# A mixing kernel for one core: the leftover group of the middle stage on 96 rows and 128 columns

## The chip, the cores and the metric

The kernel runs on one core of a Trainium2 chip. The metric is the time of one execution on the device in microseconds, of which the median over several runs is compared. The engines are named as in the profile: PE (TensorE, matmuls; PEld are its weight loads), DVE (VectorE), ACT (ScalarE), POOL (GpSimd) and SP (SyncE, which here only issues DMAs).

## What is computed

The first half is a global filter: a real Fourier transform along the sequence of 3008 positions, a product with a complex filter, and the way back, for 8 batches and 256 channels. The second half is a feed-forward layer with the activation h - tanh(h).

```
batch, seq, dim = (8, 3008, 256)          # d_ff = 2048
X = np.fft.rfft(x, axis=1)
F = (filt_r + 1j * filt_i)[None, :, :]
y = np.fft.irfft(X * F, n=x.shape[1], axis=1)
h = y.reshape(8 * 3008, 256) @ w_in
out = (h - np.tanh(h)) @ w_out
```

## The kernel before

3008 is 64 x 47, and the transform goes in stages. For every batch a *first* stage (`first`) multiplies by 64-point matrices and stores to `ct1` in HBM; a *middle* stage (`middle`) loads from `ct1`, does the 47-point transform, the filter and the 47-point way back, and stores to `ct2`; a *last* stage (`last`) loads from `ct2` and multiplies by 64-point matrices again, 128 columns a matmul, into `ut`. From there `up`, `shrink` and `down` are the feed-forward layer, whose matmuls (lines L469 and L639) are by far the most.

The middle stage has 32 slots of 24 rows each (`NA`, `NH`: frequencies of one residue), 4 planes and 256 channels. Slots are taken in groups of five, `SLOTS`, so there are six groups of 5 x 24 = 120 rows (`KM`) and one leftover group, the seventh, of 2 x 24 = 48 rows (`KL`). A group's way through the stage:

- `load_a2` and `load_ft` load its data (`a2`, line L270) and its filter rows (`ft`, L276), both on SP's queue, while the group ahead is worked on.
- `forth`: twice two matmuls (L287) of the group's matrices, as weights, with 256 columns of `a2`, into a PSUM bank `pa`; ACT copies the first bank (L290), DVE adds and subtracts (L292, L293).
- `filtered`: six DVE operations over four planes or two (L303, L318, L320, L321, L323, L324). For batch 0 some of it runs in another form (`pool` is given).
- `back`: twice two matmuls (L334) into a bank `pe`, a copy by ACT to `e1` (L337), and a store to `ct2` that ACT issues itself (L338).

The matrices lie in `mats`. For the groups of five they are block diagonal with five equal 24x24 blocks. The leftover group holds the slots 30 and 31, of which the last is the special one of the frequencies 0 and half; its eight matrices have two different blocks, and stand 48 columns wide (`KL`) behind the others. `ways` picks them.

The order of the work is written out by hand. The feed-forward runs in quarters `U`: `up` of one, `shrink` of the one before and `down` of the one before that are interleaved. Within it `up` calls `t(k)`, which puts in one step of the generators `first` and `middle` of later batches at planned positions (`planned`), and a PSUM bank of the feed-forward is borrowed for it (`zd`, bank "y" or "t"). So the matmuls of the middle stage stand singly in the stream of PE, between those of `up` and `down`. On the borrowed bank "y" they follow the DVE operation L492, which reads that bank. One batch's period is 24 such quarters.

Batch 0 isn't handled there: in the prologue its middle stage is unrolled, with `forth`, `filtered` and `back` called with the functions' 256 columns (`there0`, `ended`). The prologue also loads `mats`, its first three matrices on SP's queue and the rest with one issue on POOL's queue (L968), between the loads of the filter rows of the first two groups (`filters_of`), ahead of two small copies (`turned_rows`) and of weight loads (L143).

Of the kernel before, what the change touches and what calls it, by code (L numbers as in the profile page):

```python
# [9 lines left out]
F32 = mybir.dt.float32  # L10
# [7 lines left out]
BATCH, SEQ, DM = 8, 3008, 256  # L18
# [10 lines left out]
SLOTS = [(a, min(SG, NA - a)) for a in range(0, NA, SG)]  # L29
KM = SG * NH  # L30
KL = SLOTS[-1][1] * NH

SMALL = 0.36
FACTORS = [(0.28138768672943115, 0.18210311233997345, 0.5012423992156982),
# [12 lines left out]
def _consts():  # L47
    q = np.arange(NQ)[:, None]
    k1 = np.arange(1, NA)[None, :]

    def angle(r):
        return 2 * np.pi * ((k1 * (NR * q + r)) % SEQ) / SEQ

    def sign(r):
        return (-1.0) ** ((q[:, 0] + r) % 2)

    f = np.zeros((2, NQ, NH, 4, NA))
    g = np.zeros((4, NA, NH, 2, NQ))
    for r in range(NH):
        for half, n in ((0, r), (1, NR - r)):  # L60
            if half and not r:
                continue
            odd = 1.0 - 2 * half
            c, s = np.cos(angle(n)), np.sin(angle(n))
            f[half, :, r, 0, :-1], f[half, :, r, 1, :-1] = c, -s
            f[half, :, r, 2, :-1], f[half, :, r, 3, :-1] = -odd * s, odd * c
            plus, minus = (1 + sign(n)) / 2, (1 - sign(n)) / 2
            f[half, :, r, 0, -1], f[half, :, r, 2, -1] = plus, minus
            f[half, :, r, 1, -1], f[half, :, r, 3, -1] = odd * plus, odd * minus
            g[0, :-1, r, half], g[1, :-1, r, half] = 2 * c.T, -2 * s.T  # L70
            g[2, :-1, r, half], g[3, :-1, r, half] = -2 * odd * s.T, 2 * odd * c.T
            g[0, -1, r, half], g[2, -1, r, half] = plus, minus
            g[1, -1, r, half], g[3, -1, r, half] = odd * plus, odd * minus
    g /= SEQ

    t = 2 * np.pi * (np.outer(np.arange(NH), np.arange(NH)) % NR) / NR
    cos, sin = np.cos(t), np.sin(t)
    twice = np.where(np.arange(NH) > 0, 2.0, 1.0)[:, None]
    mats = np.zeros((KM, 6 * KM + 8 * KL))
    for k, m in enumerate((cos, sin, -sin)):  # L80
        way = np.einsum("rm,st->srmt", m, np.eye(SG))
        mats[:, k * KM:k * KM + KM] = way.reshape(KM, KM)
        mats[:, (3 + k) * KM:(4 + k) * KM] = way.reshape(KM, KM).T
    for k, (a, b) in enumerate(((cos, cos), (cos, -sin), (sin, cos), (-sin, -sin),
                                (cos, twice * cos), (cos, -2 * sin),
                                (sin, twice * cos), (-sin, -2 * sin))):
        at = 6 * KM + k * KL
        mats[0:NH, at:at + NH], mats[NH:KL, at + NH:at + KL] = a, b

    f = f[:, :, :, ORDER, :]  # L90
    return [np.ascontiguousarray(v, dtype=np.float32)
            for v in (f.reshape(128, -1), f[:, :, :, 0:2].reshape(128, -1), g.reshape(128, -1), mats, np.eye(128))]

@with_exitstack
def kernel(
# [24 lines left out]
    def dram(t, off, dims):  # L120
        return bass.AP(tensor=t, offset=off, ap=[list(d) for d in dims])

    mats = cst.tile([KM, 6 * KM + 8 * KL], F32, name="mats_sb")
    groups = [(b, c) for b in range(BATCH) for c in range(NC)]
    count = cst.tile([1, 1], I32, name="count")
    one = cst.tile([128, 128], F32, name="one_sb")

    def ways(g, back):

        if g < len(SLOTS) - 1:  # L130
            m = [mats[0:KM, (3 * back + k) * KM:(3 * back + k + 1) * KM] for k in range(3)]
            return m[0], m[0], m[1], m[2]
        at = 6 * KM + 4 * back * KL
        return [mats[0:KL, at + k * KL:at + (k + 1) * KL] for k in range(4)]

    wu = cst.tile([128, 7, DFF // 2], F32, name="wu")
    wd = cst.tile([128, 7, DFF // 2], F32, name="wd")
# [119 lines left out]
            ACT.dma_start(dram(ct1[b], XH * c * DM, [[NH * DM, 128], [1, XH * DM]]), a1)  # L257
            yield

    def rows(t, b, g, first_block=0, n=4):  # L260

        a, s = SLOTS[g]
        return dram(t[b], (first_block * NA + a) * NH * DM,
                    [[DM, s * NH], [NA * NH * DM, n], [1, DM]])

    def load_a2(b, g, tag="a2", bufs=2):

        n = SLOTS[g][1] * NH
        t = tr.tile([KM, 4, DM], F32, tag=tag, bufs=bufs, name="a2")
        nc.sync.dma_start(t[0:n], rows(ct1, b, g))  # L270
        return t

    def load_ft(g):
        n = SLOTS[g][1] * NH
        t = tr.tile([KM, 4, DM], F32, tag="ft", bufs=2, name="ft")
        nc.sync.dma_start(t[0:n], dram(filt_d, g * KM * 4 * DM, [[4 * DM, n], [1, 4 * DM]]))  # L276
        return t

    def forth(g, at, z):

        n = SLOTS[g][1] * NH
        xy = tr.tile([KM, 4, DM], F32, tag="xy", bufs=2, name="xy")[0:n]
        way = ways(g, 0)
        for v in (1, 0):
            pa = z("pa", [128, 2, DM])[0:n]
            for k in range(2):
                nc.tensor.matmul(pa[:, k], way[2 * v + k], at[0:n, PLACE[2 * v + k]],  # L287
                                 start=True, stop=True)
            if v:
                ACT.copy(xy[:, 2:4], pa)  # L290
            yield xy
        V.tensor_add(xy[:, 0:2], pa, xy[:, 2:4])  # L292
        V.tensor_sub(xy[:, 2:4], pa, xy[:, 2:4])  # L293
        yield

    def filtered(g, xy, ft, by, by2, pool=None):

        n = SLOTS[g][1] * NH
        ab = xy.rearrange("p (x v) c -> p x v c", v=2)
        fv = ft[0:n].rearrange("p (x v) c -> p x v c", v=2)  # L300
        nn = (tr.tile([128, 4, DM], F32, tag="nn", bufs=1, name="nn") if pool is None else
              pool.tile([KM, 4, DM], F32, tag="nn", bufs=3, name="nn"))[0:n]
        by.tensor_mul(nn.rearrange("p (x v) c -> p x v c", v=2), ab,  # L303
                      fv[:, :, 0:1].to_broadcast([n, 2, 2, DM]))
        yield nn
        if pool is not None:
            fi = ft[0:n, 1:4:2]
# [10 lines left out]
        by.tensor_mul(ab, ab, fv[:, :, 1:2].to_broadcast([n, 2, 2, DM]))  # L318
# [5 lines left out]
        V.tensor_sub(xy[:, 2:4], nn[:, 0:2], nn[:, 2:4])  # L324
        yield

    def back(b, g, xy, z):

        n = SLOTS[g][1] * NH
        way = ways(g, 1)  # L330
        for v in range(2):
            pe = z("pe", [128, 2, DM])[0:n]
            for k in range(2):
                nc.tensor.matmul(pe[:, k], way[2 * v + k], xy[:, 2 * v + k],  # L334
                                 start=True, stop=True)
            e1 = tr.tile([128, 2, DM], F32, tag="e1", bufs=2, name="e1")[0:n]
            ACT.copy(e1, pe)  # L337
            ACT.dma_start(rows(ct2, b, g, 2 * v, 2), e1)  # L338
            yield

    def middle(b, z):
# [495 lines left out]
    with tc.tile_pool(name="tr", bufs=2) as tr, tc.manual_schedule():  # L837
# [12 lines left out]
        with tc.tile_pool(name="pro", bufs=1) as pro, \  # L850
# [60 lines left out]

            def back0(g, nn):

                way = ways(g, 1)
                for v in range(2):
                    pe = z0("pe", [128, 2, DM])[0:KM]
                    for k in range(2):
                        nc.tensor.matmul(pe[:, k], way[2 * v + k], nn[:, k],
                                         start=True, stop=False)
                        nc.tensor.matmul(pe[:, k], way[3 - k if v else 0], nn[:, 2 + k],  # L920
                                         start=False, stop=True)
                    e1 = pro.tile([128, 2, DM], F32, tag="e1", bufs=5, name="e1")[0:KM]
                    ACT.copy(e1, pe)
                    ACT.dma_start(rows(ct2, 0, g, 2 * v, 2), e1)

            def tiles0(k, dtype, n):
                return pro.tile([128, n], dtype, tag=k, name=k,
# [37 lines left out]
            G.tensor_copy(gate, xs[1][64:65, 0, 0:1])  # L965
            began.append(begun(tiles0, jobs[2], queue=G))
            fts = {0: filters_of(0)}
            G.dma_start(mats[:, 3 * KM:], mats_d[:, 3 * KM:])  # L968
            fts[1] = filters_of(1)
            turned_rows()  # L970

            early = weights(tiles0, range(3), G, began, 3)
# [32 lines left out]
            summed = (last_g,)  # L1005

            def there0(g):
                there = forth(g, a2.pop(g), z0)
                xy = next(there)
                next(there)  # L1010
                return there, xy
# [12 lines left out]
            for g in range(last_g + 1):  # L1024
# [14 lines left out]
                    next(chain)  # L1039
                if g in summed:  # L1040
                    next(chain)
                ended.append((back, (0, g, xy, z0)) if g in summed else (back0, (g, nn)))
                if g:
                    way_back()
                if g == last_g - 1:
# [192 lines left out]
```

## Time and profile before

| what | value |
|---|---|
| median of 3 runs | 2751.55 us (2750.81 to 2753.89) |
| the profiled execution | 2753.31 us, its span 2751.4 us |
| TensorE clock granted, mean of the span | 0.996 |
| DMA queue of SP | 293981 packets, 146.89 MB, 21.9% of 16 engines |
| DMA queue of ACT | 39056 packets, 48.25 MB, 5.8% |
| matrices' load on POOL's queue | one issue, 348.8 KB, landed after 8.4 us |
| a load of the leftover group (a2, ft) | 192 KB each, 7 and 7 issues |
| a store of the leftover group | 96 KB, 16 issues (batch 0 included) |

In the profile's groups an entry names the line, the engine, the operation, what is written from what, then the shape: for a matmul first rows\*columns of the weights, then partitions x columns of the result. After the bar stand the busy time and the mean of one instruction, and after the second bar the idle time of the engine in front of it and what ended it. In a timeline a line has the start and the length in us, and how many instructions were merged (x4). Lengths of matmuls overlap, since one starts before the last has left the array; what one costs is the distance from its start to the next start.

### The profile page before, as it was taken

The page shows a single profiled execution, that of the slowest core. Times are in us where ns is not written, and L with a number is a line of the kernel's source. Part 1 is how long each engine was busy: PE and PEld are TensorE (multiplying, and loading weights), DVE is VectorE, ACT ScalarE, POOL GpSimd, SP SyncE. Part 2 cuts the span into 40 slices and gives each one's busy share as a digit, 9 for nine tenths or more (in the row PEclk, how much of TensorE's full clock was granted, in tenths as well). Part 3 has the DMA queues.
Part 4 walks back from the last instruction along what each step waited for, and adds up shares of the span by engine and source line. Part 5 has one row for each costly group of instructions (what it writes and reads, how often), then busy time and mean ns, then how long its engine had stood idle before and what let it go on. Part 6 is the DMA issues. An engine that isn't in the chain of part 4 may idle for free.

```text
span 2751.4 us, 36435 instructions
## 1 busy us (share of the span) xinstructions
PE 2706.0 (98%) x12934; PEld 2366.6 (86%) x12934; DVE 1669.0 (61%) x2082; ACT 1730.6 (63%) x2595; POOL 1296.8 (47%) x1070
## 2 busy tenths in 40 slices
PE   8899999999999999999999999999999999999998
PEld 7578889888898888988889888898888988899887
DVE  6667766666556665666646665466655666644545
ACT  3566666666666666666666666666666666666665
POOL 3115445544554454545455445455454554455452
PEclk9999999999999999999999999999999999999999
DMA  7753222331233312423233222332322221111110
GB/s 197 226 170 98 72 59 72 103 90 40 65 84 97 83 48 62 113 69 82 51 76 97 70 78 53 94 78 68 84 57 63 52 63 53 30 27 31 22 25 17
DMA packets 336508, 207.77 MB, mean 76 GB/s; under 512 B 226390, under 2 KB 299042, under 8 KB 336061
## 3 DMA queue, kind: packets, MB, share of 16 engines
q1 hardware_dynamic: 293981, 146.89, 21.9%
q10 hardware_dynamic: 39056, 48.25, 5.8%
q0 software_dynamic: 3280, 10.22, 1.3%
q8 instruction: 104, 1.70, 0.3%
q14 instruction: 87, 0.71, 0.1%
HBM read 133.31 MB, written 74.97 MB: 76 GB/s over the span
## 4 chain that ended last, share of the span: by engine, by line
PE 90%; DVE 4%; DMA 2%; issue 2%; ACT 2%; ACTq 0%; POOL 0%; SPq 0%; DVEq 0%; POOLq 0%
PE o L639 38%; PE x L469 22%; PE z L469 11%; PE y L469 5%; PE pa L287 3%; PE pu L431 3%; PE pe L334 3%; PE pf L255 2%; DMA raw<-in_moe_w_in_dram 1%; PE o L693 1%; DVE h L591 1%; DVE h L525 1%; DVE h L492 1%; DMA ct<-e 0%; DVE xy L324 0%
## 5 line engine op out<-in xcount | busy, mean ns | idle before, releaser
L639 PE MATMUL o<-t,wd 128*128 128x256 f32 (+1 forms) x3008 | 760.8, 376 | 0.0
L449 POOL TENSOR_TENSOR t<-h 128x512 f32<-128x512 f32 (+1 forms) x186 | 256.2, 1377 | 930.4 <-DVE h L591 857.7
L591 DVE TENSOR_TENSOR h<-h,y 128x1024 f32<-128x1024 f32 (+1 forms) x384 | 512.2, 1334 | 286.6 <-ACT y L587 286.0
L639 PEld LDWEIGHTS o<-t,wd 128*128 128x128 f32 x3008 | 571.3, 190 | 68.8 <-issue 2.4
L469 PE MATMUL x<-tu,wu 128*128 128x256 f32 (+1 forms) x2256 | 574.7, 377 | 1.7 <-ACT u L475 1.2
L639 PE MATMUL o<-h,wd 128*128 128x256 f32 (+1 forms) x2256 | 571.4, 376 | 1.8 <-DVE h L591 1.8
L469 PEld LDWEIGHTS x<-tu,wu 128*128 128x128 f32 x2256 | 422.3, 190 | 62.2 <-ACT u L475 9.8
L639 PEld LDWEIGHTS o<-h,wd 128*128 128x128 f32 x2256 | 424.7, 190 | 52.2 <-DVE h L591 2.6
L475 ACT COPY s<-x 128x512 f32<-128x512 f32 (+1 forms) x188 | 108.6, 578 | 501.4 <-PE x L469 486.5
L581 ACT ACTIVATE y<-h 128x1024 f32<-128x1024 f32 (+1 forms) x384 | 400.1, 1042 | 14.3 <-ACT a L256 6.7
L584 ACT ACTIVATE y<-y 128x1024 f32<-128x1024 f32 (+1 forms) x384 | 399.2, 1039 | 12.1
L587 ACT ACTIVATE y<-y 128x1024 f32<-128x1024 f32 (+1 forms) x384 | 399.9, 1041 | 5.4 <-ACT a L256 0.8
L509 DVE TENSOR_TENSOR h<-z,u 128x512 f32<-128x512 f32 (+1 forms) x188 | 127.6, 678 | 258.4 <-ACT u L475 257.3
L475 ACT COPY u<-x 128x512 f32<-128x512 f32 (+1 forms) x376 | 214.7, 571 | 86.3 <-PE x L469 65.1
L451 POOL TENSOR_TENSOR t<-h 128x512 f32<-128x512 f32 (+1 forms) x186 | 266.9, 1435 | 0.0
L450 POOL TENSOR_TENSOR t<-h,t 128x512 f32<-128x512 f32 (+1 forms) x186 | 259.7, 1396 | 14.6
L452 POOL TENSOR_TENSOR t<-h,t 128x512 f32<-128x512 f32 (+1 forms) x186 | 263.4, 1416 | 0.0
L517 DVE COPY h<-x 128x512 f32<-128x512 f32 (+1 forms) x188 | 127.9, 680 | 157.9 <-PE x L469 157.3
L469 PE MATMUL z<-ut,wu 128*128 128x256 f32 (+1 forms) x752 | 190.4, 376 | 0.0
L469 PE MATMUL z<-tu,wu 128*128 128x256 f32 (+1 forms) x752 | 190.3, 376 | 0.0
L469 PE MATMUL x<-ut,wu 128*128 128x256 f32 (+1 forms) x752 | 190.2, 376 | 0.0
L469 PE MATMUL y<-ut,wu 128*128 128x256 f32 (+1 forms) x752 | 190.1, 375 | 0.0
(145 smaller groups left out, 3086.3 us busy)
## 6 DMA issues: line engine op xcount, KB each, us to landing
e<-ct SPq DMA_DIRECT2D x48, 512.0 KB
ct<-e ACTq DMA_DIRECT2D x96, 240.0 KB
ct<-a ACTq DMA_DIRECT2D x82, 256.0 KB
a<-ct SPq DMA_DIRECT2D x42, 480.0 KB
ft<-filt SPq DMA_DIRECT2D x42, 480.0 KB
out_dram<-ot SPq DMA_DIRECT2D x1248, 16.0 KB
x_sb<-in_x_dram SPq DMA_DIRECT2D x154, 128.0 KB
gt<-g SPq DMA_DIRECT2D x48, 256.0 KB
```

Of the source, the lines that this page charges most:

```text
L449: by.tensor_sub(t[0], b[0][1], b[0][0])
L450: by.tensor_sub(t[1], b[1][1], t[0])
L451: by.tensor_sub(t[2], b[1][1], b[0][1])
L452: by.tensor_sub(t[3], b[1][0], t[1])
L469: nc.tensor.matmul(bank[:, k], wu[:, q - 1, (2 * u + k) * 128:(2 * u + k + 1) * 128], rhs[q - 1], start=(first and k == 0), stop=True, ski ...
L475: ACT.copy(t, X)
L517: V.tensor_copy(h[:, 2, :, 0:w], X)
L581: ACT.activation(y[k], ht[k], AF.Arctan, scale=TURN)
L584: ACT.activation(y[k], y[k], AF.Tanh, scale=BEND)
L587: ACT.activation(y[k], y[k], AF.Square, scale=SCALE, accum_out=y_sums[:, 2 * U + k // 2:2 * U + k // 2 + 1])
L591: V.tensor_mul(ht[k], ht[k], y[k])
L639: nc.tensor.matmul(product(q), wd[:, q - 1, (2 * u + k) * 128: (2 * u + k + 1) * 128], rhs[q - 1][:, k], start=(u == 0 and k == 0 and q == ...
```

## The change

The leftover group of the batches 1 to 7 is laid out anew: the first 128 channels stand on 48 rows as before, and the second 128 channels on 48 further rows below. So its tiles have 96 rows (`KH`) and 128 columns instead of 48 and 256. Its matrices become 96x96 with the old 48x48 twice on the diagonal. Batch 0 keeps the old form (`whole`) with the upper left quarter of the new matrices. Each load of `a2` and `ft` and each store of `e1` of this group is issued in two halves of 128 channels, of 512 bytes a run. The load of the matrices on POOL's queue is split: the three matrices of the way back of the groups of five first, the leftover group's eight, now 96 rows of 768 columns, after the second group's filter rows. The number and the order of matmuls stay.

The core of the diff (lines of `_consts`, the helpers, the prologue):

```diff
+KH = 2 * KL
...
-    mats = np.zeros((KM, 6 * KM + 8 * KL))
+    mats = np.zeros((KM, 6 * KM + 8 * KH))
...
-        at = 6 * KM + k * KL
-        mats[0:NH, at:at + NH], mats[NH:KL, at + NH:at + KL] = a, b
+        for row in (0, KL):
+            at = 6 * KM + k * KH + row
+            mats[row:row + NH, at:at + NH] = a
+            mats[row + NH:row + KL, at + NH:at + KL] = b
...
+    def extent(g, whole):
+
+        n = SLOTS[g][1] * NH
+        return (n, DM) if whole or g < len(SLOTS) - 1 else (2 * n, DM // 2)
...
-        at = 6 * KM + 4 * back * KL
-        return [mats[0:KL, at + k * KL:at + (k + 1) * KL] for k in range(4)]
+        at = 6 * KM + 4 * back * KH
+        return [mats[0:n, at + k * KH:at + k * KH + n] for k in range(4)]
...
+    def parts(t, b, g, whole, first_block=0, n=4):
 
         a, s = SLOTS[g]
-        return dram(t[b], (first_block * NA + a) * NH * DM,
-                    [[DM, s * NH], [NA * NH * DM, n], [1, DM]])
+        rows, w = s * NH, extent(g, whole)[1]
+        for h in range(DM // w):
+            yield (slice(rows * h, rows * (h + 1)), w,
+                   dram(t[b], (first_block * NA + a) * NH * DM + w * h,
+                        [[DM, rows], [NA * NH * DM, n], [1, w]]))
...
-        nc.sync.dma_start(t[0:n], rows(ct1, b, g))
+        for rows, w, src in parts(ct1, b, g, False):
+            nc.sync.dma_start(t[rows, :, 0:w], src)
...
-        nc.sync.dma_start(t[0:n], dram(filt_d, g * KM * 4 * DM, [[4 * DM, n], [1, 4 * DM]]))
+        for h in range(DM // w):
+            nc.sync.dma_start(t[rows * h:rows * (h + 1), :, 0:w],
+                              dram(filt_d, g * KM * 4 * DM + w * h,
+                                   [[4 * DM, rows], [DM, 4], [1, w]]))
...
-                nc.tensor.matmul(pa[:, k], way[2 * v + k], at[0:n, PLACE[2 * v + k]],
+                nc.tensor.matmul(pa[:, k], way[2 * v + k], at[0:n, PLACE[2 * v + k], 0:w],
...
-            ACT.copy(e1, pe)
-            ACT.dma_start(rows(ct2, b, g, 2 * v, 2), e1)
+            ACT.copy(e1[0:n], pe)
+            for rows, _, dst in parts(ct2, b, g, whole, 2 * v, 2):
+                ACT.dma_start(dst, e1[rows])
...
-            G.dma_start(mats[:, 3 * KM:], mats_d[:, 3 * KM:])
+            G.dma_start(mats[:, 3 * KM:6 * KM], mats_d[:, 3 * KM:6 * KM])
             fts[1] = filters_of(1)
+            G.dma_start(mats[0:KH, 6 * KM:], mats_d[0:KH, 6 * KM:])
             turned_rows()
```

In `filtered` and `back` the tiles are cut to `n` rows and `w` columns in the same way.

More of the change, by code (lines that the diff above doesn't have):

```diff
@@ L121, in dram @@
         return bass.AP(tensor=t, offset=off, ap=[list(d) for d in dims])
-    mats = cst.tile([KM, 6 * KM + 8 * KL], F32, name="mats_sb")
+    mats = cst.tile([KM, 6 * KM + 8 * KH], F32, name="mats_sb")
     groups = [(b, c) for b in range(BATCH) for c in range(NC)]
@@ L126, with ways @@
     one = cst.tile([128, 128], F32, name="one_sb")
-    def ways(g, back):
+    def extent(g, whole):
+        n = SLOTS[g][1] * NH
+        return (n, DM) if whole or g < len(SLOTS) - 1 else (2 * n, DM // 2)
+    def ways(g, back, n):
         if g < len(SLOTS) - 1:
@@ L258, in first, with forth @@
             yield
-    def rows(t, b, g, first_block=0, n=4):
+    def parts(t, b, g, whole, first_block=0, n=4):
         a, s = SLOTS[g]
-        return dram(t[b], (first_block * NA + a) * NH * DM,
-                    [[DM, s * NH], [NA * NH * DM, n], [1, DM]])
+        rows, w = s * NH, extent(g, whole)[1]
[3 more added lines that the diff above has]
+                        [[DM, rows], [NA * NH * DM, n], [1, w]]))
     def load_a2(b, g, tag="a2", bufs=2):
-        n = SLOTS[g][1] * NH
         t = tr.tile([KM, 4, DM], F32, tag=tag, bufs=bufs, name="a2")
-        nc.sync.dma_start(t[0:n], rows(ct1, b, g))
+        for rows, w, src in parts(ct1, b, g, False):
+            nc.sync.dma_start(t[rows, :, 0:w], src)
         return t
     def load_ft(g):
-        n = SLOTS[g][1] * NH
+        n, w = extent(g, False)
+        rows = SLOTS[g][1] * NH
         t = tr.tile([KM, 4, DM], F32, tag="ft", bufs=2, name="ft")
-        nc.sync.dma_start(t[0:n], dram(filt_d, g * KM * 4 * DM, [[4 * DM, n], [1, 4 * DM]]))
-        return t
[L279 to L283, printed above, removed]
+        for h in range(DM // w):
+            nc.sync.dma_start(t[rows * h:rows * (h + 1), :, 0:w],
+                              dram(filt_d, g * KM * 4 * DM + w * h,
+                                   [[4 * DM, rows], [DM, 4], [1, w]]))
+        return t
+    def forth(g, at, z, whole=False):
+        n, w = extent(g, whole)
+        xy = tr.tile([KM, 4, DM], F32, tag="xy", bufs=2, name="xy")[0:n, :, 0:w]
+        way = ways(g, 0, n)
         for v in (1, 0):
-            pa = z("pa", [128, 2, DM])[0:n]
+            pa = z("pa", [128, 2, DM])[0:n, :, 0:w]
             for k in range(2):
-                nc.tensor.matmul(pa[:, k], way[2 * v + k], at[0:n, PLACE[2 * v + k]],
+                nc.tensor.matmul(pa[:, k], way[2 * v + k], at[0:n, PLACE[2 * v + k], 0:w],
                                  start=True, stop=True)
@@ L296, in filtered @@
     def filtered(g, xy, ft, by, by2, pool=None):
-        n = SLOTS[g][1] * NH
+        n, w = extent(g, pool is not None)
         ab = xy.rearrange("p (x v) c -> p x v c", v=2)
-        fv = ft[0:n].rearrange("p (x v) c -> p x v c", v=2)
+        ft = ft[0:n, :, 0:w]
+        fv = ft.rearrange("p (x v) c -> p x v c", v=2)
         nn = (tr.tile([128, 4, DM], F32, tag="nn", bufs=1, name="nn") if pool is None else
-              pool.tile([KM, 4, DM], F32, tag="nn", bufs=3, name="nn"))[0:n]
+              pool.tile([KM, 4, DM], F32, tag="nn", bufs=3, name="nn"))[0:n, :, 0:w]
         by.tensor_mul(nn.rearrange("p (x v) c -> p x v c", v=2), ab,
-                      fv[:, :, 0:1].to_broadcast([n, 2, 2, DM]))
+                      fv[:, :, 0:1].to_broadcast([n, 2, 2, w]))
         yield nn
         if pool is not None:
-            fi = ft[0:n, 1:4:2]
+            fi = ft[:, 1:4:2]
             V.tensor_mul(xy[:, 1:3], xy[:, 1:3], fi)
@@ L317, in filtered @@
             return
-        by.tensor_mul(ab, ab, fv[:, :, 1:2].to_broadcast([n, 2, 2, DM]))
+        by.tensor_mul(ab, ab, fv[:, :, 1:2].to_broadcast([n, 2, 2, w]))
         yield
@@ L325, in filtered, with back @@
         yield
-    def back(b, g, xy, z):
-        n = SLOTS[g][1] * NH
-        way = ways(g, 1)
+    def back(b, g, xy, z, whole=False):
+        n, w = extent(g, whole)
+        way = ways(g, 1, n)
         for v in range(2):
-            pe = z("pe", [128, 2, DM])[0:n]
+            pe = z("pe", [128, 2, DM])[0:n, :, 0:w]
             for k in range(2):
@@ L335, in back @@
                                  start=True, stop=True)
-            e1 = tr.tile([128, 2, DM], F32, tag="e1", bufs=2, name="e1")[0:n]
-            ACT.copy(e1, pe)
-            ACT.dma_start(rows(ct2, b, g, 2 * v, 2), e1)
+            e1 = tr.tile([128, 2, DM], F32, tag="e1", bufs=2, name="e1")[:, :, 0:w]
+            ACT.copy(e1[0:n], pe)
+            for rows, _, dst in parts(ct2, b, g, whole, 2 * v, 2):
+                ACT.dma_start(dst, e1[rows])
             yield
@@ L912, in back0 @@
             def back0(g, nn):
-                way = ways(g, 1)
+                way = ways(g, 1, KM)
                 for v in range(2):
@@ L923, in back0 @@
                     ACT.copy(e1, pe)
-                    ACT.dma_start(rows(ct2, 0, g, 2 * v, 2), e1)
+                    ACT.dma_start(next(parts(ct2, 0, g, True, 2 * v, 2))[2], e1)
             def tiles0(k, dtype, n):
@@ L1007, in there0 @@
             def there0(g):
-                there = forth(g, a2.pop(g), z0)
+                there = forth(g, a2.pop(g), z0, True)
                 xy = next(there)
@@ L1041 @@
                     next(chain)
-                ended.append((back, (0, g, xy, z0)) if g in summed else (back0, (g, nn)))
+                ended.append((back, (0, g, xy, z0, True)) if g in summed else (back0, (g, nn)))
                 if g:
```

## The prediction

> **What bounds the kernel now.** I read the page first, then the groups with different shapes kept apart, then PE's timeline around the instructions that the change touches, and last the waits. The page:
>
> ```profile
> span 2751.4 us, 36435 instructions
> PE 2706.0 (98%) x12934; PEld 2366.6 (86%) x12934; DVE 1669.0 (61%) x2082; ACT 1730.6 (63%) x2595; POOL 1296.8 (47%) x1070
> PE 90%; DVE 4%; DMA 2%; issue 2%; ACT 2%; ACTq 0%; POOL 0%; SPq 0%; DVEq 0%; POOLq 0%
> ```
>
> TensorE is the bound: busy 98% of the span and 90% of the chain, no other engine over 63%. So an edit is worth what it takes from PE's stream of matmuls, plus what it takes from a wait of PE. The groups by form:
>
> ```profile
> L431 PE MATMUL pu<-gt,e 128*128 128x128 f32 x736 | 99.2, 278 | 4.2 <-DMA e<-ct 4.2
> L334 PE MATMUL pe<-xy,mats_sb 48*48 48x256 f32 x64 | 16.8, 385 | 1.0 <-DVE h L492 1.0
> L287 PE MATMUL pa<-a,mats_sb 48*48 48x256 f32 x64 | 16.8, 385 | 3.0 <-DVE h L492 3.0
> L324 DVE TENSOR_TENSOR xy<-nn 48x512 f32<-48x512 f32 x7 | 11.2, 1604 | 0.0
> L653 DVE TENSOR_TENSOR o<-o,p 128x256 f32<-128x256 f32 x40 | 17.0, 425 | 54.2 <-ACT p L652 54.2
> ```
>
> Each f32 matmul leaves two records: 64 of the 48-row form on each line are 8 batches x 4 matmuls x 2. The mean of 385 ns is latency; matmuls overlap, so cost is read from start to start. A 256-column group, a 120-row group of the middle stage, and the 128-column matmuls of the last stage, on PE's timeline:
>
> ```profile
> 959.72 1.03 PE L287 MATMUL pa<-a,mats_sb 120*120 120x256 f32 x4
> 960.58 1.03 PE L469 MATMUL x<-tu,wu 128*128 128x256 f32 x4
> 961.45 1.24 PE L639 MATMUL o<-t,wd 128*128 128x256 f32 x5
> ...
> 982.28 1.03 PE L469 MATMUL y<-ut,wu 128*128 128x256 f32 x4
> 983.14 1.05 PE L431 MATMUL pu<-gt,e 128*128 128x128 f32 x8
> 984.03 1.25 PE L639 MATMUL o<-h,wd 128*128 128x256 f32 x5
> ```
>
> Four records of 256 columns take 0.86 us, 216 ns each, 120 rows or 128. Eight of 128 columns take 0.89 us, 111 ns each. Now one leftover group (48 rows) in the stream:
>
> ```profile
> 1010.96 1.03 PE L469 MATMUL x<-ut,wu 128*128 128x256 f32 x4
> 1011.82 1.03 PE L469 MATMUL y<-ut,wu 128*128 128x256 f32 x4
> 1012.78 0.59 PEld L287 LDWEIGHTS pa<-a,mats_sb 48*48 48x48 f32 x4 [0.33 <-issue]
> 1012.78 1.06 PE L287 MATMUL pa<-a,mats_sb 48*48 48x256 f32 x4
> 1013.77 1.59 PEld L639 LDWEIGHTS o<-h,wd 128*128 128x128 f32 x8 [0.40 <-issue]
> 1013.77 2.00 PE L639 MATMUL o<-h,wd 128*128 128x256 f32 x8
> ...
> 1015.60 0.59 PE L469 MATMUL x<-tu,wu 128*128 128x256 f32 x2
> ```
>
> The y group before it takes 0.96 instead of 0.86, the group itself 0.99 instead of 0.86, and the eight records behind it 1.83 instead of 8 x 0.216 = 1.73. That is 0.33 us lost though nothing is waited for; record by record it is 0.325 us in every undisturbed leftover group. The weight loads stand still at both edges (0.33 and 0.40 "issue"), which they don't around the 120-row group. In the prologue eight transposes of form 128\*48 (128 rows, 48 columns) follow each other at 109 ns without such a gap, so the few rows cost it, not the few columns.
>
> The Trainium skill, page "TensorEngine Tiling (Array Packing)", section "Tiling Modes", says that the array can be split at 64 rows for small contractions and that changing the mode drains it. The gaps at both edges of 48 rows agree with that; by its list of modes 96 rows need the whole array, as 120 do.
>
> **The change part by part.** Seven batches x 4 groups (two L287, two L334) = 28 groups of 4 records, 112 records, turn from 48 rows x 256 columns to 96 x 128; their order on PE stays.
>
> (a) Columns: 112 x (216 - 111) ns = 11.7 us less. The 111 is from full 128x128 loads, the nearest row above; the shorter 96-column load (48\*48 loads take 119 ns on average, 120\*120 loads 183 to 186) can't be worse.
>
> (b) The edges: 28 x 0.325 = 9.1 us less if 96 rows behave like 120. No row shows 96; bounds are 0 (like 48) and 9.1 (like 120). I take 9.1, since the 120-row group lies nearer and the loss goes with rows. A correction: six of the groups start behind a DVE wait (once near 359 us, then near 666, 1001, 1336, 1671, 2006). There the wait hides the edge in front, and a 120-row group behind a wait shows its first load exposed (314 instead of 216 ns), so these save 0.13 instead of 0.325: -1.1 us.
>
> (c) DVE and one wait. The leftover group's DVE operations fall from 1024 and 512 elements a row to half. In five batches PE waits before the first back group:
>
> ```profile
> 1055.06 1.76 DVE L324 TENSOR_TENSOR xy<-nn 48x512 f32<-48x512 f32 x1
> 1056.75 0.67 DVE L492 TENSOR_TENSOR h<-y,s 128x512 f32<-128x512 f32 x1
> 1057.48 1.06 PE L334 MATMUL pe<-xy,mats_sb 48*48 48x256 f32 x4 [0.20 <-DVE h L492]
> ```
>
> L492 frees the bank, and it queues behind the group's L323 (0.67) and L324 (1.76). At 256 elements an undisturbed operation takes 0.425 (L653); L324 is stretched beside POOL's L450 and L451, by 1.76 / 0.68 = 2.6 over its undisturbed length, so at worst it becomes 0.425 x 2.6 = 1.1. L492 then starts at least (0.67 + 1.76) - (0.425 + 1.1) = 0.9 us earlier, more than the wait: the record in front lasts 585 ns there and 309 at an edge without a wait, 0.276 us. Five times: 1.4 us less. Bounds 0 and 1.4. The rest of what DVE gains, some 4 us a batch, pays nothing: no PE wait ends there. The waits near 971 and 1001 us (0.87 and 0.68) hang on 120-row operations and stay.
>
> (d) ACT. Per batch three copies shrink (0.58 to about 0.37, L652's 128x256), and each of the two stores becomes two issues: 14 more of 0.33 us. Behind the added issue on ACT stands the copy L475 of u (1059.64 to 1060.23), which the next matmuls into x (1062.02) wait for: 1.8 us of cover against 0.33 - 0.21 = 0.12 us. Without cover 14 x 0.33 = 4.6 us. Behind the prologue 98 such stores are issued; 96 start 0.03 us after their copy, two wait longer (0.49 and 1.79 us, at 260 and 270, while SP moves the filter rows). I take 0.
>
> (e) Loads on SP: a2 and ft of the group in two issues each, 14 more of 0.33 to 0.5 us, and runs of 512 B instead of 1 KB and 4 KB. They are issued a whole group ahead (at 942 and 947 for matmuls from 1001 on), and SP's queue mostly waits for its next store. The e2 load of the next batch waits for the group's stores: issued at 1069.18, first used at 1094, cover 25 us. 0; bounds 0 and 1 us a batch.
>
> (f) Prologue: the matrices' load on POOL's queue is split, its second part put behind batch 0's second filter, and grows from 349 KB in all to 169 + 288 = 457 KB. One POOL issue more (0.8 us) stands ahead of the two turned rows and two weight loads; POOL then sits idle 8.9 us until 43.47, and the new part is first needed near 68 us. I take 0; bounds -0.5 (the first part lands earlier) to 2 us.
>
> Sum: 11.7 + 9.1 - 1.1 + 1.4 = 21.1 us less. The first copy x of the next half after a group was free 3.0 us before it was written (1012.60 against 1015.60), so 0.75 us off a group doesn't run into ACT.
>
> The profiled execution took 2753.3 us with a span of 2751.4; the median of the three runs is 2751.55. The span should fall to 2730.3, the median to **2730.5**.
>
> **The rivals.** *The edges stay.* If the array is changed over for 96 rows too, (b) is gone: 11.7 + 1.4 = 13.1, or 2738.4. For it: no 96-row matmul is shown. Against it: 120 rows, which don't fill the array either, pay nothing.
>
> *Weight loads bind.* A load takes up to 190 ns; were each to last that long on the path, a record would cost 190, not 111: 112 x 79 ns = 8.8 us less gain, 2739.3. Against it stand 736 records of L431 at 111 ns with such loads. The Trainium skill, page "TensorE: Matmul & The Clock Gate", section "Back-to-back issue gap", gives 81 ns per 128-column matmul when loads alternate, against 56 for the array alone. By that a two-pass record would take an estimated 162 ns and the gain shrink by 5.7 us; the trace's 111 is twice the smaller figure and disagrees.
>
> *Slower.* ACT issues in order, and in the built program each DMA of SP and ACT takes the next of eight completion semaphores in turn and waits for the landing of its last user. Doubled stores reach one issue deeper into SP's queue. SP's issues have stood up to 5.5 us for an earlier landing. If each of the 14 added stores held ACT so long, 1.8 covered, PE would lose 14 x 3.7 = 52 us: 2751.5 - 21.1 + 52 = 2782. It decides from 14 x 1.5 = 21 us, a hold of 3.3 us each. For it: the two stores near 260 and 270 that did wait. Against it: 96 of 98 don't, and none of a leftover group did.
>
> *It doesn't do what it says.* Then 2751.5. The changed program's PE order has 28 x 2 matmuls of 96x128 in place of 48x256, so hardly.
>
> **How the numbers follow.** Forecast 0.81 (own range 2727 to 2735: knock-on waits of some 4 us either way), edges stay 0.08, loads bind 0.04, slower 0.04, no effect 0.03. 0.2% is 5.5 us, about what a measurement here can tell from nothing. The first three are faster by more: 0.93; same 0.03; slower 0.04. The range runs from 2727 to 2741, over both smaller gains.
>
> **What would show it.** L287 and L334 with form 96\*96, 128 columns, four records in about 0.45 us from start to start, and no 0.33 or 0.40 "issue" at PEld around them: (a) and (b) right. Gaps of 0.1 us at their edges: the edges stay. About 190 ns a record: loads bind. No PE wait for L492 before the first back group: (c). ACT idle ahead of the ct2 stores: the slower rival. I'm wrong if the period of 335.1 us from batch to batch falls by less than 2 us, or if the first 95 us grow by over 2.

## The result, and the profile after

| what | before | changed |
|---|---|---|
| median of 4 runs | 2751.18 us (2750.24 to 2753.89) | 2731.13 us (2729.91 to 2731.80) |
| profiled execution | 2753.31 us, span 2751.4 | 2729.91 us, span 2728.0 |

The ratio is 0.9925, with a 95% interval from 0.9908 to 0.9942: 20.05 us or 0.73% less, against 21.1 us and a median of 2730.5 in the prediction. Every line of the changed kernel stands some 15 to 17 further down: L302 and L350 are the matmuls that were L287 and L334, L486 and L656 the feed-forward (L469, L639), L339 and L340 the last two DVE operations of a group (L323, L324), L509 the sum that frees bank "y" (L492), L353 and L355 the copy and the store of `e1` (L337, L338), L492 the copy of u (L475), L448 the last stage's matmul (L431).

The page of the changed kernel, its engines and the chain of waits:

```profile
PE 2684.1 (98%) x12934; PEld 2364.1 (87%) x12934; DVE 1650.7 (61%) x2082; ACT 1725.3 (63%) x2595; POOL 1282.2 (47%) x1071
PE 91%; DVE 4%; issue 2%; ACT 1%; DMA 1%; ACTq 0%; POOL 0%; SPq 0%; DVEq 0%; POOLq 0%
```

TensorE is still the bound, with the same 12934 records, and its busy time fell by 21.9 us (2706.0 to 2684.1) where the span fell by 23.4. The new form of the forward matmuls and their loads, from the groups with shapes kept apart (the back ones have the same count):

```profile
L302 PE MATMUL pa<-a,mats_sb 96*96 96x128 f32 x56 | 8.9, 281 | 3.4 <-DVE h L509 3.4
...
L302 PEld LDWEIGHTS pa<-a,mats_sb 96*96 96x96 f32 x56 | 7.1, 162 | 6.4 <-DVE h L509 5.8
```

PE's timeline around the leftover group that stood at 1012.78 before:

```profile
1003.41 1.03 PE L486 MATMUL y<-ut,wu 128*128 128x256 f32 x4
1004.06 0.60 PEld L302 LDWEIGHTS pa<-a,mats_sb 96*96 96x96 f32 x4
1004.27 0.60 PE L302 MATMUL pa<-a,mats_sb 96*96 96x128 f32 x4
...
1004.71 1.89 PE L656 MATMUL o<-h,wd 128*128 128x256 f32 x8
1006.44 0.81 PE L486 MATMUL x<-tu,wu 128*128 128x256 f32 x3
```

Both effects can be read from the starts. The group takes 0.44 us (1004.27 to 1004.71) where it took 0.99. The y group in front is back at 0.86 us (0.96 before), the eight records behind are back at 1.73 (1.83 before), and PEld carries no "issue" gap at either edge, where it had 0.33 and 0.40. The mean load of 96 columns takes 162 ns and lies beside the matmuls.

Both traces have the same 12934 matmul records in the same order, so they can be set against each other record by record. The 28 leftover groups, each measured from the start of the record ahead of it to the start of the third record behind it:

| groups of a kind | before | changed | less, each | predicted | less in all |
|---|---|---|---|---|---|
| 17 without a wait | 1.835 us | 1.090 us | 0.745 | 0.745 | 12.7 us |
| 5 forward, behind the wait for the sum | 2.43 | 1.85 | 0.58 | 0.55 | 2.9 |
| 1 forward, near 359 us | 2.27 | 2.13 | 0.14 | 0.55 | 0.1 |
| 5 first back groups, whose wait goes | 2.115 | 1.090 | 1.02 | 1.02 | 5.1 |

That is 20.8 us, and it is what the stream lost: from the start of the 701st record to the end of the span the two profiled executions differ by 20.70 us (2567.97 against 2547.27). "In the stream" stands for this stretch below. The other 2.7 us between the two spans lie ahead of that record and are not put down to the change, for the reasons given with terms (e) and (f).

### The profile page after: what moved, and what is told of

Same layout as the page of the kernel before. It is cut to its first block, busy times and chain, and to the rows that moved or that the text cites. A ratio compares the mean times of both kernels' runs of the same rounds, so it can differ in the third digit from the quotient of the medians.

```text
span 2728.0 us, 36466 instructions
## 1 busy us (share of the span) xinstructions
PE 2684.1 (98%) x12934; PEld 2364.1 (87%) x12934; DVE 1650.7 (61%) x2082; ACT 1725.3 (63%) x2595; POOL 1282.2 (47%) x1071
## 4 chain that ended last, share of the span: by engine, by line
PE 91%; DVE 4%; issue 2%; ACT 1%; DMA 1%; ACTq 0%; POOL 0%; SPq 0%; DVEq 0%; POOLq 0%
PE o L656 38%; PE x L486 23%; PE z L486 11%; PE y L486 5%; PE pa L302 3%; PE pu L448 3%; PE pe L350 3%; PE pf L263 2%; DMA raw<-in_moe_w_in_dram 1%; PE o L710 1%; DVE h L608 1%; DVE h L542 0%; DVE h L509 0%; DVE xy L340 0%; ACT y L598 0%
## 5 line engine op out<-in xcount | busy, mean ns | idle before, releaser
L656 PE MATMUL o<-t,wd 128*128 128x256 f32 (+1 forms) x3008 | 759.7, 375 | 0.0
L466 POOL TENSOR_TENSOR t<-h 128x512 f32<-128x512 f32 (+1 forms) x186 | 253.9, 1365 | 931.9 <-DVE h L608 856.8
L656 PEld LDWEIGHTS o<-t,wd 128*128 128x128 f32 x3008 | 570.5, 190 | 67.2
L486 PE MATMUL x<-tu,wu 128*128 128x256 f32 (+1 forms) x2256 | 573.1, 376 | 1.2 <-ACT u L492 0.8
L656 PE MATMUL o<-h,wd 128*128 128x256 f32 (+1 forms) x2256 | 570.4, 375 | 1.8 <-DVE h L608 1.8
L486 PEld LDWEIGHTS x<-tu,wu 128*128 128x128 f32 x2256 | 421.6, 190 | 57.0 <-ACT u L492 9.4
L656 PEld LDWEIGHTS o<-h,wd 128*128 128x128 f32 x2256 | 424.2, 190 | 50.3 <-DVE h L608 2.6
L492 ACT COPY s<-x 128x512 f32<-128x512 f32 (+1 forms) x188 | 108.7, 578 | 501.5 <-PE x L486 480.8
L492 ACT COPY u<-x 128x512 f32<-128x512 f32 (+1 forms) x376 | 214.9, 572 | 83.5 <-PE x L486 56.8
L469 POOL TENSOR_TENSOR t<-h,t 128x512 f32<-128x512 f32 (+1 forms) x186 | 262.7, 1413 | 0.0
L468 POOL TENSOR_TENSOR t<-h 128x512 f32<-128x512 f32 (+1 forms) x186 | 262.7, 1413 | 0.0
L467 POOL TENSOR_TENSOR t<-h,t 128x512 f32<-128x512 f32 (+1 forms) x186 | 255.8, 1375 | 14.6
L486 PE MATMUL x<-ut,wu 128*128 128x256 f32 (+1 forms) x752 | 190.2, 375 | 0.0
L486 PE MATMUL z<-ut,wu 128*128 128x256 f32 (+1 forms) x752 | 190.1, 375 | 0.0
L486 PE MATMUL z<-tu,wu 128*128 128x256 f32 (+1 forms) x752 | 190.0, 375 | 0.0
L486 PE MATMUL y<-ut,wu 128*128 128x256 f32 (+1 forms) x752 | 190.0, 375 | 0.0
```

The costliest lines, as they stand in the source:

```text
L466: by.tensor_sub(t[0], b[0][1], b[0][0])
L467: by.tensor_sub(t[1], b[1][1], t[0])
L468: by.tensor_sub(t[2], b[1][1], b[0][1])
L469: by.tensor_sub(t[3], b[1][0], t[1])
L486: nc.tensor.matmul(bank[:, k], wu[:, q - 1, (2 * u + k) * 128:(2 * u + k + 1) * 128], rhs[q - 1], start=(first and k == 0), stop=True, ski ...
L492: ACT.copy(t, X)
```

## Experiments

Each experiment is the changed kernel with one edit. Times are medians; the ratio is to the kernel before, run beside it on the same chip.

### Rows alone, and columns alone

Two kernels split the saving between its two terms. In the first the rows are doubled and the 256 columns kept; both halves of the rows hold the same data (the loads and stores are cut to match, which isn't shown):

```diff
-        return (n, DM) if whole or g < len(SLOTS) - 1 else (2 * n, DM // 2)
+        return (n, DM) if whole or g < len(SLOTS) - 1 else (2 * n, DM)
```

> 96 rows, but 256 columns as before: both row halves hold the same whole data, and the first 48 rows are stored. PE keeps 112 records of 216 ns. Theory (the edges of a matmul on few rows cost 0.325 us a group, and 96 rows pay none): no gap at the edges; 28 x 0.325 less 11 groups behind a DVE wait x 0.19, so 7.0 us under the kernel before, about 2744. Rival (the whole gain comes from the columns, the edges follow from something else in the old form): 2751. Rival (the relief of DVE is what pays): 2751 too, since DVE's operations keep their width.

Measured: 2744.79 us (2743.03 to 2746.48), ratio 0.9976 (0.9966 to 0.9987), 6.6 us less than the kernel before; from the 701st record on 6.97 us less. The group on PE's timeline:

```profile
1009.40 1.03 PE L302 MATMUL pa<-a,mats_sb 96*96 96x256 f32 x4
1010.26 1.89 PE L656 MATMUL o<-h,wd 128*128 128x256 f32 x8
```

The y group in front starts at 1008.54, so the starts are 0.86 us apart on both sides, and the length behind is 1.89 instead of 2.00: 96 rows pay no edge. By the prediction's prices the 17 groups without a wait save 17 x 0.325 and the 11 behind one 11 x 0.13, since the five first back groups still wait here: 6.96 us.

In the second the rows stay at 48, and only 128 columns are multiplied; it leaves out the second half of the channels of this group, and their loads:

```diff
-        return (n, DM) if whole or g < len(SLOTS) - 1 else (2 * n, DM // 2)
+        return (n, DM) if whole or g < len(SLOTS) - 1 else (n, DM // 2)
```

> 48 rows as before, but 128 columns: the leftover group's second half of the channels is left out (the first half's result is stored in both places). Theory: 112 records at 111 ns, edges of 0.325 us stay around each of the 28 groups, the PE wait before the first back group goes: 11.7 + 1.4 = 13.1 us under before, about 2738. Rival (columns pay nothing because weight loads or edges fill the time): 2750.

Measured: 2739.16 us (2735.41 to 2739.50), ratio 0.9953 (0.9940 to 0.9967); 12.53 us less in the stream.

```profile
1006.39 1.03 PE L488 MATMUL y<-ut,wu 128*128 128x256 f32 x4
1007.35 0.63 PE L304 MATMUL pa<-a,mats_sb 48*48 48x128 f32 x4
1007.91 1.99 PE L658 MATMUL o<-h,wd 128*128 128x256 f32 x8
```

Here the y group is stretched to 0.96 again and the group takes 0.56 where the 96-row one takes 0.44. Over the undisturbed groups the loss is 0.317 us, close to the 0.325 of 256 columns. So the edge doesn't go with the length of the matmul, and the two terms nearly add up: 6.97 + 12.53 = 19.5 us, against 20.70 for both. Of the 1.2 us between, 0.9 is the five first back groups, whose edge in front is hidden by their wait in the first of the two kernels, and 0.3 the group near 359 us.

In all these kernels the weights have as many columns as rows (48\*48, 96\*96), so few columns of the weights could be meant as well. Against that stand the transposes that the prediction names, in the kernel before:

```profile
61.58 1.04 PE L894 MATMUL pq<-one_sb,wd 128*48 128x128 f32 x8
62.45 0.60 PE L287 MATMUL pa<-a,mats_sb 120*120 120x256 f32 x2
```

Their weights have 128 rows and 48 columns, and 120-row matmuls stand on both sides. The 120-row record ahead starts 216 ns earlier, and the eight take 0.87 us, 109 ns each up to the next start: neither edge is paid. So it is the few rows that cost it. Only a weight of 128 rows and a single column (128\*1, at 2739.36 us) also starts 309 ns after the record ahead; what holds between 1 and 48 columns no run shows.

### At how many rows the edge begins

Two kernels, one run each, have 64 and 72 rows and 256 columns. The added rows hold a copy of some of the 48; the loads are cut to match, which isn't shown:

```diff
-        return (n, DM) if whole or g < len(SLOTS) - 1 else (2 * n, DM // 2)
+        return (n, DM) if whole or g < len(SLOTS) - 1 else (64, DM)
```

> The form of 256 columns with 64 rows (48 and a copy of 16 of them), to place the edge. Theory (64 rows and less are taken as half the array, and the change to it and back costs the edge): 0.325 us around each group as with 48 rows, time near 2751. Rival (each missing strip of 32 rows, or any number of rows under 120, costs): the same here, told apart by 72 rows.

> The same with 72 rows (48 and a copy of 24). Theory: no edge, as with 96, time near 2744. Rival (the loss grows as rows fall): an edge between 0 and 0.325 us.

Measured: 2752.97 us with 64 rows and 2742.73 with 72. PE's timeline with 64 rows:

```profile
1011.04 1.03 PE L487 MATMUL y<-ut,wu 128*128 128x256 f32 x4
1012.00 1.07 PE L303 MATMUL pa<-a,mats_sb 64*64 64x256 f32 x4
1013.00 1.99 PE L657 MATMUL o<-h,wd 128*128 128x256 f32 x8
```

With 64 rows the starts are 0.96 and 1.00 us apart and the length behind is 1.99, as with 48; with 72 rows the starts are 0.87 and 0.86 us apart and that length is 1.89; over the undisturbed groups the loss is 0.338 us with 64 and 0.005 with 72. The limit lies above 64 rows and at or below 72.

### The wait before the first back group

Term (c) held that five waits go because the leftover group's last DVE operations halve. So the last one is done twice:

```diff
-        V.tensor_sub(xy[:, 2:4], nn[:, 0:2], nn[:, 2:4])
+        for _ in range(1 + (g == len(SLOTS) - 1)):
+            V.tensor_sub(xy[:, 2:4], nn[:, 0:2], nn[:, 2:4])
```

> The changed kernel with the leftover group's last DVE subtraction done twice (same result), which puts one more operation of 0.41 to 1.5 us in front of the sum that frees bank y. Theory (the wait before the first back group went only because DVE's operations got shorter, with 0.2 us to spare in the trace): the wait is back in five batches at 0.2 to 1.4 us each with an exposed first load of 0.08, so 2732.5 to 2738.5, and the profile shows it at the 96x96 back matmuls. Rival (PE's wait there went for another reason, or DVE has cover): 2731.

Measured: 2736.00 us (2735.37 to 2739.20), ratio 0.9943 (0.9928 to 0.9958); 6.34 us more in the stream than the changed kernel. From the waits of PE (us in all, times, longest):

```profile
PE pe L351 <- DVE h L510: 11.8, 10, 1.3
```

In the changed kernel the same entry has 6.3 us in 5 places. Five places became ten again, as before the change, with 5.5 us more of waiting. The waits are longer than those that went (the record ahead of the group lasts 1.47 us, 0.59 before the change), since a whole operation was added. The wait that went was DVE's, and it hung on what stands ahead of the sum in DVE's queue.

### The loads and the stores

The load of the matrices on POOL's queue is put together again:

```diff
-            G.dma_start(mats[:, 3 * KM:6 * KM], mats_d[:, 3 * KM:6 * KM])
+            G.dma_start(mats[:, 3 * KM:], mats_d[:, 3 * KM:])
             fts[1] = filters_of(1)
-            G.dma_start(mats[0:KH, 6 * KM:], mats_d[0:KH, 6 * KM:])
```

> The changed kernel with the matrices of POOL's queue in one issue again, at the old place, 541 KB. Theory (the prologue's 2.7 us in the changed kernel's profile are the phase of the TensorE clock and not the split): same time as the changed kernel within 1 us, about 2731. Rival (the split brings the prologue forward): 2733 to 2734.

Measured: 2731.40 us (2729.65 to 2735.34), ratio 0.9931 (0.9917 to 0.9944), and 2547.24 us from the 701st record on, against 2547.27: the split is worth nothing.

The stores of the leftover group are doubled once more, one plane of `e1` an issue:

```diff
-            for rows, _, dst in parts(ct2, b, g, whole, 2 * v, 2):
-                ACT.dma_start(dst, e1[rows])
+            for k in range(2):
+                for rows, _, dst in parts(ct2, b, g, whole, 2 * v + k, 1):
+                    ACT.dma_start(dst, e1[rows, k:k + 1])
```

(for this group alone; the others keep one issue)

> The changed kernel with each store of the leftover group in four issues on ACT instead of two (512-byte runs as before), 28 issues more. Theory (ACT's issues lie beside PE's work): 2731 to 2732, and no PE wait for an ACT copy behind the stores. Rival (ACT's queue sets the end there, or stores wait for a completion semaphore): 28 x 0.4 = 11 us more, about 2742, with ACT idle ahead of the added stores.

Measured: 2741.15 us (2740.64 to 2743.05), ratio 0.9963 (0.9949 to 0.9976): 10.0 us above the changed kernel. My theory fell. The rival's 2742 agrees with the time by luck, since its price of 0.4 us an added issue isn't what was paid. The timeline of ACT, its queue and PE around one of them:

```profile
1721.75 3.56 ACTq L360 DMA_DIRECT2D ct<-e  x4
...
1725.40 0.58 ACT L497 COPY u<-x 128x512 f32<-128x512 f32 x1 [3.68 <-DMA ft<-filt]
...
1726.04 1.85 PE L491 MATMUL x<-tu,wu 128*128 128x256 f32 x4 [1.94 <-ACT u L497]
```

The four issues hold ACT for 3.56 us, but no issue is slow in itself: the first three start at 1721.75, 1722.12 and 1722.59 and take 0.34 to 0.43 us each, and the fourth starts only at 1724.98 and takes 0.32. In between ACT stands 1.95 us for the landing of a load of the filter rows (`ft`) that SP issued at 1718.13. In the trace the DMAs of SP and ACT take eight completion semaphores in turn, and the fourth store has the one of that load (113). This is the mechanism of the prediction's slower rival. It comes once in each of four batches, with a wait of 1.5 to 2.0 us. Of the ten other stores in four issues nine are done in 1.74 to 1.76 us and one, near 394 us, in 2.63.

The copy of u starts only behind the last issue, and PE stands 1.94 us for it. In these four batches PE needs 9.15 to 11.24 us from one back group to the other instead of 7.35, and 7.75 in two more; over the whole run it waits for that copy 8.7 us in 8 places, against 0.8 us in 2 in the changed kernel. In the place shown TensorE's clock falls as well: it is granted at 0.54 between 1726.04 and 1729.60, and there records of 256 columns follow at 427 ns instead of 216, some 1.7 us more. Behind the three other pauses of 1.7 to 2.1 us the clock stays at 1.00.

Why the changed kernel doesn't pay yet, its timeline shows at the same place:

```profile
1713.64 0.80 ACTq L355 DMA_DIRECT2D ct<-e  x2
1714.54 0.59 ACT L492 COPY u<-x 128x512 f32<-128x512 f32 x1 [0.93 <-ACT e L353]
1715.83 1.03 PE L486 MATMUL x<-tu,wu 128*128 128x256 f32 x4
```

Two issues take 0.80 us, the copy of u ends at 1715.13, and PE writes x at 1715.83: 0.70 us of cover are left. None of its 14 second issues stands for a landing.

### The waits that remain

After the change 14.2 us of PE's waits hang on L509, the DVE sum that reads bank "y": 7.9 us ahead of forward groups and 6.3 ahead of back groups, the longest entries of the view:

```profile
PE pa L302 <- DVE h L509: 7.9, 12, 1.0
PE pe L350 <- DVE h L509: 6.3, 5, 1.3
```

Two ways to be rid of them were tried on top of the change. One issues the sum on DVE ahead of the middle stage's step, so that it queues behind less of that step's work:

```diff
+        V.tensor_add(h[:, 0, :, 0:w], Y, s1)
         t(0)
         d()
         shrinks(0)
-        V.tensor_add(h[:, 0, :, 0:w], Y, s1)
```

> The changed kernel with the sum of Y and s1 issued on DVE ahead of the planned step t(0), so that no DVE operation of the middle stage stands in front of it; PE's order is unchanged. The changed kernel's profile has 14.2 us of PE idle until that sum, in 17 places, each with an exposed first load of some 0.09 us. Theory (these waits are the order of DVE's queue and nothing else): they go, 2715 to 2717. Rival (DVE's operations of the middle stage, now behind a sum that waits for ACT, come late themselves and PE waits for them or for the adds behind them): 2727 to 2735.

Measured: 2727.69 us (2727.36 to 2729.10), ratio 0.9915 (0.9902 to 0.9929), only 3.4 us below the changed kernel. My theory fell, and the time lies in the rival's range. DVE's timeline ahead of a forward group shows why most of the waits stay:

```profile
958.55 1.75 DVE L340 TENSOR_TENSOR xy<-nn 120x512 f32<-120x512 f32 x1
...
960.83 0.68 DVE L506 TENSOR_TENSOR h<-y,s 128x512 f32<-128x512 f32 x1
961.56 1.12 PE L302 MATMUL pa<-a,mats_sb 120*120 120x256 f32 x4 [0.71 <-DVE h L506]
```

L340, and L339 ahead of it (956.92, 1.71 us), were issued in a step of the quarter before, so they stand ahead of the sum wherever the sum is put within its own quarter. 6.3 us of waits in five places and 3.5 us in five more remain. What the rival feared is there too, in a small way: L339 of the leftover group now runs behind the sum, and each of the five first back groups waits for it and takes 1.54 us, measured as in the table, where the changed kernel has 1.09: 2.2 us in all.

The other way lets the step t(1) borrow the other bank, "t", so that its group no longer waits for that sum:

```diff
-                latest[0] = "y" if quarter[0] in (1, 2, 3) and latest[0] == "t" else "t"
+                latest[0] = "y" if quarter[0] in (2, 3) and latest[0] == "t" else "t"
```

> The changed kernel with one condition of the bank choice altered: at the second planned step of a quarter, t(1), the borrowed bank is t instead of y. Theory (the 14.2 us of PE idle in the changed kernel end when bank y is read by the sum behind DVE's queue, and t is free by then, since its copy ended 0.5 us or more before): those waits go and with them the exposed first loads, 2715 to 2719. Rival (t's reader of the step before is late in as many places): 2728 to 2735, with PE waiting for ACT copies or DVE in their place.

Measured: 2715.48 us (2714.09 to 2716.51), ratio 0.9867 (0.9850 to 0.9883), 15.6 us below the changed kernel, and 17.99 us below it in the stream. On its page DVE's share of the chain of waits falls from 4% to 1% and PE's rises from 91% to 95%. No wait of a forward or back group for that sum is left; only the wait for ACT's copy of u grows, from 0.8 us in 2 places to 2.1 in 4. Both edits together:

> The same choice of bank together with the sum issued ahead of t(0). Theory: with no one waiting for bank y at t(1) the order of the sum no longer matters, and the 0.4 us in front of the first back group that the order brought stays: 2716 to 2721, no better than the bank alone. Rival (both gains add): 2712 or less.

Measured: 2718.29 us (2717.34 to 2719.84), ratio 0.9881 (0.9864 to 0.9897): no better than the bank alone. Nothing is left for the earlier sum to save, and it brings back what it cost: the five first back groups wait for L339 again and take 1.54 us instead of 1.09, 2.2 us in all, and the stream is 2.15 us longer than with the bank alone. The version with the bank alone is the fastest of the study. What the bank's edit would be worth in the kernel before was not tried.

## Why the prediction came out right

**(a) The columns, 11.7 us.** Right, by records: within a group the starts now follow at 113, 109, 108 and 109 ns where 111 was taken from the 128-column matmuls of the last stage. The 128 columns alone on 48 rows took 12.5 us off, which includes the five first back waits; 12.53 less 1.4 leaves 11.1 for the columns; what is short of 11.7 is mostly the group near 359 us, which saves nothing there.

**(b) The edges, 9.1 less 1.1 us.** Right: 0.745 a group against 0.420 + 0.325, and rows alone came to 6.97 us, where these prices give 6.96. The choice between the bounds, by the 120-row group, held. The Trainium skill, page "TensorEngine Tiling (Array Packing)", section "Tiling Modes", lists modes of 64 and of 32 rows beside the whole array, and says that a change of mode drains it. The kernels with 64 and 72 rows agree with a limit at 64. That a plain matmul on few rows is run in such a mode is not shown, and what such a visit costs, here 0.32 to 0.34 us for its two edges, only these runs show.

The correction for six groups behind a wait was right in kind. Five of them saved 0.58 us each, near the 0.420 + 0.13 = 0.55 of the prediction. The sixth, near 359 us, saved only 0.14. In the changed kernel's timeline there:

```profile
354.16 1.76 DVE L340 TENSOR_TENSOR xy<-nn 120x512 f32<-120x512 f32 x1
...
356.58 0.68 PE L302 MATMUL pa<-a,mats_sb 96*96 96x128 f32 x4 [0.80 <-DVE h L509]
```

L340 of the 120-row group before sets when L509 runs. DVE doesn't get faster there, so what PE gained on the way is given back in a wait that is 0.44 us longer. The prediction named this wait as one that hides an edge, and overlooked that it also takes back what PE gained just ahead of it.

**(c) The five waits, 1.4 us.** Right in size: 1.02 us of these groups each, against 0.745 of the others, is 0.276 more, and the doubled operation brought the waits back. Its working was too hopeful. Before the first back group:

```profile
1045.64 1.50 DVE L340 TENSOR_TENSOR xy<-nn 96x256 f32<-96x256 f32 x1
...
1047.06 0.68 DVE L509 TENSOR_TENSOR h<-y,s 128x512 f32<-128x512 f32 x1
1047.95 0.60 PE L350 MATMUL pe<-xy,mats_sb 96*96 96x128 f32 x4
```

L340 takes 1.50 us beside POOL, where 1.1 was called the worst. The prediction stretched an operation in proportion to its length, and the traces show another pattern: such an operation ends a fixed time behind the instruction that POOL has running, as if it waited for it. L340 here ends at 1047.14, 0.28 us behind the end of POOL's L467 (1046.86); before the change L324, with 512 elements, ended 0.55 us behind POOL's L450. So do L339 and L340 of all 120-row groups of the changed kernel wherever an instruction of POOL is still running at their start, whether they take 0.9 us or 1.8. With POOL idle the two lengths take 0.41 and 0.68 us. So halving the elements takes only some 0.27 us off such an operation, and the sum comes earlier by 0.53 us against PE's stream, not 0.9. It ends at 1047.74, 0.21 us ahead of the group. The term came out whole with little to spare, and in that it was lucky.

**(d) ACT's stores, 0.** Right as a sum, with the margin mis-sized. Some 1.7 us of cover were to be left; 0.70 are. The second issue took 0.47 us where 0.33 was taken, and PE arrives earlier while the copy of `e1` is held by other work of ACT. The slower rival put the danger on this queue and was not met in the changed kernel. With four issues in place of two its mechanism came, a store that waits for an earlier landing, but once in each of four batches and not at every added store: 10 us and not the 52 worked out for it.

**(e) SP's loads, 0, and (f) the prologue, 0.** The stream from the 701st record on has no loss to put to the loads: the groups' 20.8 us account for its 20.70. The split load made no difference either. What the profile shows ahead of that record, 183.45 us before and 180.72 after, goes with TensorE's granted clock. Before, the mean clock was 1.00 between 60 and 80 us and 0.83 between 80 and 100; after, 0.91 and 1.00. The kernel with the doubled DVE operation has the prologue of the changed one, and comes to the same record at 183.68 us, with 1.00 and 0.83. In the twelve profiles TensorE runs at half clock for 10.2, 13.7 or 17.1 us ahead of that record, and the record starts at 180.47 to 181.71 us in the four with 10.2, at 181.16 to 183.68 in the six with 13.7, and at 184.03 and 185.32 in the two with 17.1. The changed kernel has 10.2, the kernel before 13.7. So these 2.7 us aren't put down to the change; the medians' 20.05 us agree with the stream's 20.70 without them. Why the clock differs there was not tried.

**The rivals.** *The edges stay* is refuted by the 96-row groups, with and without 256 columns, and would have been right with 64 rows. *Weight loads bind* is refuted by 108 to 113 ns a record with loads of 162 ns: the load of the next runs beside the matmul. The Trainium skill, page "TensorE: Matmul & The Clock Gate", section "Back-to-back issue gap", gives 81 ns a 128-column matmul when loads alternate, by which the prediction estimated 162 ns a record; the 108 to 113 ns measured here don't agree. The period from batch to batch fell from 335.08 to 331.99 us, by more than the 2 us that would have made the prediction wrong.

## What to carry to other kernels

In a stream of whole-array f32 matmuls, look for the ones on few rows: each visit with 48 or 64 rows cost 0.32 to 0.34 us here without any wait in the profile, read only from starts and from "issue" at the weight loads, and folding columns into rows (to 96 here; 72 paid nothing either) takes it away and shortens the matmul too. Then read which engine frees the PSUM bank of each small group: a bank whose reader queues behind other work cost more (15.6 us) than either half of this change. A split store is only free while its issuing engine has slack: two issues were hidden with 0.70 us left, and of four the last met a load that hadn't landed, which cost 10 us.

## What the runs showed that was not expected

- ACT's issues behind one copy took 0.33 us for one, 0.80 for two and 1.74 to 1.76 for four, but 3.15 to 3.57 in the four places where the last had to wait for the landing of an earlier load.
- A DVE operation of 256 elements a row took 0.41 us with POOL idle and 1.50 (L340) beside POOL, against 1.76 for 512 elements: it ended a fixed time behind POOL's instruction, 0.28 us with 256 elements and 0.55 with 512.
- One pause of PE of 1.94 us was followed by 3.4 us at half clock, three others of 1.7 to 2.1 us were not.
- The first 701 records took between 180.47 and 185.32 us from kernel to kernel, with a granted clock between 80 and 100 us from 0.83 to 1.00, two of these kernels (183.68 and 180.72 us) having the same prologue.
